# Two spectral and mixer layers in one kernel: a new written-out order of work, one more row summed on ScalarE, smaller first loads

## The chip, the cores and the metric

The kernel runs on one core of a Trainium2 chip. Its engines are TensorE (PE, with its weight loads PEld), VectorE (DVE), ScalarE (ACT), GpSimd (POOL) and SyncE (SP), which here only issues DMAs. The metric is device time of one execution in microseconds (us), the median of several runs.

## The reference

x is 2048 rows of 512 numbers in bfloat16. Two layers, A then B's block, are applied twice with the same weights:

```python
def _A_ref(x, w_r, w_i):
    X = rfft2(x.astype(float32), axes=(-2, -1))
    X = X * (w_r + 1j * w_i)
    return irfft2(X, s=(S, D), axes=(-2, -1)).astype(bfloat16)

def _B_ref(x, w1, w2, w3, w4):
    h = gelu(layernorm(x) @ w1)            # four quarters of h are shifted by -1, +1, -2, +2 rows
    x1 = x + shifted(h) @ w2
    return x1 + gelu(layernorm(x1) @ w3) @ w4      # 512 -> 1792 -> 512

for _ in range(2):
    x = x + _A_ref(layernorm(x), w_r, w_i)
    x = x + _B_ref(layernorm(x), w1, w2, w3, w4)
```

## The kernel before

Everything stays on the chip: `x_state` holds x as 128 partitions by 16 "rows" of 512 (a row here is one of the 16 values of q, with one sequence position in each partition). The Fourier transforms are matmuls with constant tables. One layer runs through these stages, each a letter in the written-out order, with a number for the row, pair or block, `.k` for the PSUM bank, and a last letter for the engine where there is a choice (A ScalarE, V or D VectorE, P GpSimd):

- Front: `s` statistics of a row, `i` their aggregation, `f` the same from sums made on ScalarE, `S` and `J` the root and its inverse, `Q` the table T times one over the deviation of a row (tile `Tq`), `O` the first transform (L403), `G` and `L` its copy to the tile `V`.
- Spectral part over 16 blocks b: `d` a transform (L544 to L550), `t` its copy (tile `TV`), `q` a transform whose matmuls use 64 rows of the array (L568), `x` its copy (tile `X`), `p` the product with the filter W (tile `PB`; from `X`, or with D straight from PSUM), `b` and `V` the way back (L598), `m` and `l` the copies to `hT`.
- Rest of the inverse: `D` and `C` (L618), `Y` the copy, `P` (L646), `a` the addition to x (L654), `s` squares on ScalarE, then `r`, `e`, `i`, `M` for the next normalization, `n` the normalized row, `T` the DMA that transposes two rows (L674, tile `xT`).
- Mixer: `v` the product with w1 (L686), `h` its Gelu (L693), `u` the product with w2 (L702), `f` the addition, `k` squares, `R`, `o`, `U` the second normalization and its transposing DMA, `w` the product with w3 (L737), `g` its Gelu (L744), `W` the product with w4 (L757), `A` the addition (L763), `y` the store. While the first layer's `W` runs, `B`, `j`, `S`, `Q`, `O`, `G`, `I` already make the second layer's front.
- `X` is a number of matmuls on zeros that keep TensorE going; 30 of them (L262) open the program.

The order is written out by hand in three strings: `ORDER_0` (first front), `ORDER_A` (first layer with the front of the second) and `ORDER_B` (second layer). The program is made in that order, and each engine runs its own instructions in it; semaphores hold an instruction until its operands are there and its buffer or bank is free. The tiles `TV` and `Y` share four buffers, `X` has three, `Tq` eight.

Loads: SP issues x in eight pieces of two rows, then sixteen pieces of W. ScalarE issues the table T and two small strided pieces of W ahead of its first table load. GpSimd issues FL, TL and TR after the `f` of group 2, then, after the last `Q`, four copies W to W (`double(0)` to `double(3)`), the computation of half of TL's second plane (`turn_TL`, L238 and L239), the rest of TL and the second half of TR. SP then waits for the last of these through a small DMA (`gate2`, L209) and loads G, Tinv, w1, w2, w3 and w4, one DMA each, followed by a transposing DMA of zeros (L512). DMAs from SP and ScalarE take eight completion semaphores in turn, so one issued as the ninth waits until the first has landed.

`ON_ACT` lists the rows whose sums ScalarE makes in the first front: two activations with an accumulator (L353, L290) in place of one `bn_stats` (L278) and one `bn_aggr` (L306) on VectorE, followed by three small GpSimd instructions (L359 to L361).

Of the kernel before, what the change touches and what calls it, by code (L numbers as in the profile page):

```python
# [16 lines left out]
P = 128  # L17
# [3 lines left out]
NQ = 16  # L21
# [135 lines left out]
def load_all(K, A_x, A_w_r, A_w_i, B_w1, B_w2, B_w3, B_w4):  # L157
# [11 lines left out]
    table("T", nc.scalar)  # L169
    for h in range(8):  # L170
        nc.sync.dma_start(K.x[:, h * 2:h * 2 + 2, :], xv[:, h * 2:h * 2 + 2, :])
    K.W = K.const.tile([P, 2, NH, 257], BF16, name="W")
    planes = [w.rearrange("(m j) f -> m j f", j=64) for w in (A_w_r, A_w_i)]
    for pl, v in enumerate(planes):
        nc.scalar.dma_start(K.W[2::4, pl, 0], v[:, 32])
    for lo in range(0, NH, 8):
        for pl, v in enumerate(planes):
            load_W(K, v, pl, lo, lo + 8)
# [28 lines left out]
    def load_mlp():  # L207
# [4 lines left out]
        for k, w, n, c in (("w1", B_w1, 4, D), ("w2", B_w2, 4, D), ("w3", B_w3, 4, FH), ("w4", B_w4, 14, D)):  # L212
            t = K.const.tile([P, n, c], BF16, name=k)
            nc.sync.dma_start(t[:], w.rearrange("(t p) n -> p t n", p=P))
# [164 lines left out]
def scaled_T(K, q, r, eng="V"):  # L379

    K.Tq[q] = K.stream.tile([P, 2, P], BF16, name="Tq", bufs=8)
    if eng in "VP":
        e = K.nc.vector if eng == "V" else K.nc.gpsimd
        e.tensor_scalar(K.Tq[q][:], K.T[:], r, None, op0=ALU.mult)
    else:
        K.nc.scalar.activation(K.Tq[q][:], K.T[:], ACT.Copy, bias=0.0, scale=r)  # L386
# [137 lines left out]
def layer(K, last):  # L524
# [264 lines left out]
    def scale_T(n, eng):  # L789
        k, i = divmod(n, 4) if n < 12 else (n, 0)  # L790
        scaled_T(K, ROWS[n], lnA[k].r[:, i:i + 1], eng)
# [54 lines left out]
ON_ACT = [5, 9]  # L846
# [16 lines left out]
s1 s0 i1 i0 S0 s2 s5 J0 Q0A Q1A s4 s7 s6 i4 f2 O0.4 i7 i6 S2 s3 J2 i2 s9 Q6V Q7V O3.0 i3 s11 S1 J1 s10 Q4A Q2A Q5A G3A  # L863
s8 i11 i10 i8 s12 f3 O2.2 Q3P O1.6 S3 J3 Q11P s13 i12 Q10A O5.0 s15 G0A i13 Q8A Q9P S4 G2A s14 i15 J4 Q12V i14 O4.4 S5
J5 Q15V G1A G5V Q13P O6.2 L5A O8.0 Q14V O7.6 G4A G6V G7A L7A G8V L6V L8V
"""
ORDER_A = """
d2.2 t2V d0.6 t0A d1.0 d4.4 N0 q0.6 t1A q2.2 d6.0 x0V p0V q1.6 t4A q4.4 x2A d10.2 t6A d8.0 p1D b1.6 p2P t10A b0.7
q10.2 p4D m0V t8A q6.0 d14.4 m1A d12.6 x10A t14V p10V x6A d15.2 t12A p6V b2.5 b4.3 m4A q14.0 q12.6 x14A q8.3 p12D b3.0
m2A b10.1 b11.5 x8A b7.4 t15A p14P q15.2 b5.6 b14.7 m10A b6.1 m11A b12.5 m7A m5A m3A b13.4 m6A p8V b8.6 m12A p15D b9.0  # L870
m8A b15.2 m15A V12.1 m13V V13.3 l12A m14V V15.4 V14.5 m9V l15V D3.0 l14V D1.6 l13A C1 C3 D0.2 C0 Y1A P3.4 P2.5 Y0A Y3V
a3 s3 P6.0 a2 s2 P1.1 P0.6 a1 a0 s1 P7.2 D2.4 C2 D5.6 s0 a7 s7 D7.2 C5 Y2V P5.1 r0 e0 i0 a6 Y5A a5 D4.4 s6 s5 P4.0 M0
# [61 lines left out]
```

## Time and profile before

| | us |
|---|---|
| median of 3 runs | 345.87 (345.47 to 346.12) |
| profiled execution | 346.01 |
| its span, first to last instruction | 344.2 |
| TensorE busy in the span | 335.5 |
| ScalarE busy | 195.6 |
| VectorE busy | 165.0 |
| GpSimd busy | 107.1 |

The span is 1.81 us shorter than the execution; this part lies around the instructions. Busy time of TensorE contains the zero matmuls, and the ends of matmuls are modelled. The granted TensorE clock of the execution is 1.000. A "wait" of an engine is idle time put down to the semaphore that came last.

### The profile page before, as it was taken

How to read it: one execution, taken by the hardware profiler on the slowest of the kernel's cores; microseconds unless marked ns; L12 is line 12 of the kernel's file. 1: busy time of each engine (PE TensorE's matmuls, PEld its weight loads, DVE VectorE, ACT ScalarE, POOL GpSimd, SP SyncE). 2: the span in 40 equal slices, each digit the busy share in tenths (PEclk: the TensorE clock that was granted, in tenths of full speed). 3: DMA queues.
4: the chain of work that ended last, by engine and by line, in shares of the span. 5: the costliest groups of instructions: out<-in, count | busy, mean ns of one | idle time of the engine just before them, and what ended most of it. 6: DMA issues, size and time to landing. Idle time of an engine off the chain costs nothing.

```text
span 344.2 us, 5699 instructions
## 1 busy us (share of the span) xinstructions
PE 335.5 (97%) x2171; PEld 187.6 (55%) x2189; DVE 165.0 (48%) x377; ACT 195.6 (57%) x357; POOL 107.1 (31%) x200
## 2 busy tenths in 40 slices
PE   7999999999999999999999999999999999999996
PEld 5878974444444444454467888444444444444443
DVE  4889895685035015264676979647802000110122
ACT  4979899768752403534538979968681446014300
POOL 2884066668242000304011404765591000000000
PEclk9999999999999999999999999999999999999999
DMA  7986986333030100300000002541403500000121
GB/s 257 314 295 230 372 202 113 72 61 62 3 61 0 32 0 0 31 2 0 2 0 2 2 3 47 104 81 20 89 0 76 109 0 0 30 18 5 41 78 46
DMA packets 45259, 24.60 MB, mean 71 GB/s; under 512 B 35072, under 2 KB 42240, under 8 KB 45232
## 3 DMA queue, kind: packets, MB, share of 16 engines
q1 hardware_dynamic: 43760, 19.74, 23.5%
q0 software_dynamic: 1232, 4.40, 3.7%
q8 instruction: 17, 0.28, 0.3%
q10 hardware_dynamic: 240, 0.10, 0.1%
q14 instruction: 10, 0.08, 0.1%
HBM read 11.61 MB, written 2.10 MB: 40 GB/s over the span
## 4 chain that ended last, share of the span: by engine, by line
PE 87%; DMA 4%; DVE 4%; ACT 2%; issue 1%; SPq 0%; POOL 0%; ACTq 0%; DVEq 0%; POOLq 0%
PE ps L737 28%; PE ps L757 26%; PE ps L686 8%; PE ps L702 8%; PE ps L598 4%; PE ps L403 3%; PE ps L618 3%; PE ps L568 2%; DMA xT<-xn 2%; PE ps L550 2%; PE ps L646 2%; DMA x_state<-in_A_x_dram 1%; DVE x_state L654 1%; ACT xn L290 1%; ACT gT L744 1%
## 5 line engine op out<-in xcount | busy, mean ns | idle before, releaser
L744 ACT ACTIVATE gT<-ps 128x1024 bf16<-128x1024 f32 x56 | 55.8, 1022 | 86.1 <-PE ps L737 86.1
L737 PE MATMUL ps<-xT,w 128*128 128x512 bf16 x448 | 99.2, 379 | 0.5 <-DMA xT<-xn 0.5
L757 PE MATMUL ps<-w,gT 128*128 128x512 bf16 (+2 forms) x462 | 97.8, 366 | 0.7
L763 DVE TENSOR_TENSOR x_state<-ps,x_state 128x512 bf16<-128x512 f32 (+2 forms) x34 | 22.2, 659 | 124.5 <-PE ps L757 124.5
L757 PEld LDWEIGHTS <-gT 128*128 128x128 bf16 x476 | 45.5, 98 | 51.4
L737 PEld LDWEIGHTS <-w 128*128 128x128 bf16 x448 | 43.7, 98 | 53.1 <-DMA xT<-xn 1.0
L710 DVE SCALAR_TENSOR_TENSOR xn<-xn,ln_c,ps 128x512 bf16<-128x512 bf16 x32 | 23.0, 743 | 15.5 <-PE ps L702 8.8
L686 PE MATMUL ps<-xT,w 128*128 128x512 bf16 x128 | 28.9, 379 | 0.7 <-DMA xT<-xn 0.4
L702 PE MATMUL ps<-w,hT 128*128 128x512 bf16 x124 | 28.3, 379 | 0.2
L290 ACT ACTIVATE junk<-xn 128x512 bf16<-128x512 bf16 x32 | 19.7, 622 | 4.8 <-DVE xn L710 4.8
L278 DVE BATCH_NORM_STATS2 ln_st<-x_state 128x6 f32<-128x512 bf16 (+2 forms) x31 | 20.2, 663 | 3.9 <-DMA x_state<-in_A_x_dram 3.6
L654 DVE SCALAR_TENSOR_TENSOR x_state<-ps,x_state 128x512 bf16<-128x512 f32 x32 | 20.7, 684 | 1.3 <-PE ps L646 1.2
L686 PEld LDWEIGHTS <-w 128*128 128x128 bf16 x128 | 12.3, 98 | 15.9 <-issue 1.7
L702 PEld LDWEIGHTS <-hT 128*128 128x128 bf16 x128 | 12.4, 98 | 15.3 <-ACT hT L693 0.4
L290 ACT ACTIVATE xn<-x_state 128x512 bf16<-128x512 bf16 x32 | 19.8, 620 | 0.9 <-DVE x_state L654 0.7
L693 ACT ACTIVATE hT<-ps 128x512 bf16<-128x512 f32 x32 | 17.4, 601 | 4.6 <-PE ps L686 4.4
L313 POOL TENSOR_SCALAR ln_ve<-ln_mv 128x4 f32<-128x4 f32 x11 | 2.8, 257 | 54.6 <-DVE ln_mv L306 53.9
L646 PE MATMUL ps<-Y,Tinv 128*128 128x256 bf16 x128 | 16.0, 272 | 0.1
L598 PE MATMUL ps<-TR,PB 128*128 128x128 bf16 x256 | 16.0, 219 | 0.0
L584 DVE TENSOR_TENSOR PB<-ps,W 128x1024 bf16<-128x1024 f32 x13 | 15.4, 1217 | 0.7 <-PE ps L568 0.5
L618 PE MATMUL ps<-G,hT 128*128 128x256 bf16 x128 | 15.7, 272 | 0.0
L403 PE MATMUL ps<-Tq,x_state 128*128 128x256 bf16 (+1 forms) x160 | 14.0, 246 | 1.6 <-ACT Tq L386 1.0
(95 smaller groups left out, 405.9 us busy)
## 6 DMA issues: line engine op xcount, KB each, us to landing
w<-in_B_w_dram SPq DMA_DIRECT2D x2, 1792.0 KB, 14.3
W<-W POOLq DMA_DIRECT2D x4, 514.0 KB, 5.0
x_state<-in_A_x_dram SPq DMA_DIRECT2D x8, 256.0 KB, 4.7
out_dram<-x_state SPq DMA_DIRECT2D x15, 128.0 KB, 1.9
w<-in_B_w_dram SPq DMA_DIRECT2D x2, 512.0 KB, 6.2
W<-in_A_w_r_dram SPq DMA_DIRECT2D x7, 128.5 KB, 5.8
W<-in_A_w_i_dram SPq DMA_DIRECT2D x7, 128.5 KB, 5.9
TL<-tab_TL POOLq DMA_DIRECT2D x3, 256.0 KB, 5.4
```

The source lines that it names most:

```text
L290: K.nc.scalar.activation(out, src, ACT.Square, bias=0.0, scale=D ** -0.5, accum_out=self.s[:, i, 1:2])
L403: K.nc.tensor.matmul(dst, lhsT=K.x[:, q, c * P:(c + 1) * P], rhs=rhs, start=(j == 0), stop=(j == 3))
L598: nc.tensor.matmul(o[:, k0 * P:(k0 + 1) * P], lhsT=pab[u][:, k, 2 * (b - u) + h, f * P:(f + 1) * P], rhs=K.TR[:, k:k + 2, 2 * b + h], star ...
L618: nc.tensor.matmul(o[:, i, e * 256:(e + 1) * 256], lhsT=M[:, F, e, 2 * m + i, :], rhs=K.G[:, F, e, :], start=(F == 0 and e == 0), stop=(F ...
L646: nc.tensor.matmul(o[:, h * 256:(h + 1) * 256], lhsT=K.Tinv[:, c], rhs=rhs[:, ::-1] if h else rhs, start=(e == 0), stop=(e == 1))
L654: nc.vector.scalar_tensor_tensor(K.x[:, q, :], ps.pop(("P", q)), 1.0, K.x[:, q, :], op0=ALU.mult, op1=ALU.add, accum_out=ln[g].s[:, i, 0:1])
L686: nc.tensor.matmul(o[:, i], lhsT=K.w1[:, t, j * P:(j + 1) * P], rhs=xT[g][:, :, t, :], start=(t == 0), stop=(t == 3))
L702: nc.tensor.matmul(o, lhsT=K.hT[:, j, st:st + P], rhs=K.w2[:, j, :], start=(j == 0), stop=(j == 3))
L710: nc.vector.scalar_tensor_tensor(xn[:, q, :], xn[:, q, :], ln[q // 4].c[:, q % 4:q % 4 + 1], ps.pop(("u", n)), op0=ALU.mult, op1=ALU.add, ...
L737: nc.tensor.matmul(o[:, i], lhsT=K.w3[:, c, t * P:(t + 1) * P], rhs=xT3[g][:, :, c, :], start=(c == 0), stop=(c == 3))
L744: nc.scalar.activation(gT[g][:, 2 * j:2 * j + 2, :], ps.pop(("w", k)), ACT.Gelu_apprx_tanh, bias=0.0, scale=1.0)
L757: nc.tensor.matmul(o, lhsT=gT[g][:, t, i * P:(i + 1) * P], rhs=K.w4[:, t, d], start=(t == 0), stop=(t == 13))
```

## The change

- x comes in nine pieces: rows 0 and 1 by a DMA each, then pairs.
- The table T is issued by ScalarE after the two strided pieces of W, no longer before them.
- w1, w3 and w4 are loaded in two DMAs each; w2 in one.
- Row 1's sums are made on ScalarE (`ON_ACT` gains 1), so group 0 has an `f` too.
- In the second layer's front, rows whose transform is done without folding (`PLAIN`, the first twelve) need T only with one sign: `Tq` is 128 wide there in place of 256.
- All three orders are written anew. The matmuls are the same, but for the zero matmuls at the head of `ORDER_B`: six in place of three.

```diff
-    table("T", nc.scalar)
-    for h in range(8):
-        nc.sync.dma_start(K.x[:, h * 2:h * 2 + 2, :], xv[:, h * 2:h * 2 + 2, :])
+    for lo, hi in ((0, 1), (1, 2), *((h, h + 2) for h in range(2, NQ, 2))):
+        nc.sync.dma_start(K.x[:, lo:hi, :], xv[:, lo:hi, :])
...
         nc.scalar.dma_start(K.W[2::4, pl, 0], v[:, 32])
+    table("T", nc.scalar)
...
-            nc.sync.dma_start(t[:], w.rearrange("(t p) n -> p t n", p=P))
+            v = w.rearrange("(t p) n -> p t n", p=P)
+            for part in ((slice(0, n),) if k == "w2" else (slice(0, n // 2), slice(n // 2, n))):
+                nc.sync.dma_start(t[:, part], v[:, part])
...
-    K.Tq[q] = K.stream.tile([P, 2, P], BF16, name="Tq", bufs=8)
+    K.Tq[q] = K.stream.tile([P, signs, P], BF16, name="Tq", bufs=8, padded_shape=[P, 2, P])
...
-        scaled_T(K, ROWS[n], lnA[k].r[:, i:i + 1], eng)
+        scaled_T(K, ROWS[n], lnA[k].r[:, i:i + 1], eng, 1 if n < 2 * PLAIN else 2)
...
-ON_ACT = [5, 9]
+ON_ACT = [1, 5, 9]
```

The stretches of the orders that the prediction speaks of, before (-) and after (+):

```diff
 ORDER_0
-s1 s0 i1 i0 S0 s2 s5 J0 Q0A Q1A s4 s7 s6 i4 f2 O0.4 i7 i6 S2 s3 J2 i2 s9 Q6V Q7V O3.0
+s0 s1 i0 s5 s2 s3 s4 i3 i2 f0 S0 S1 i4 J0 Q0A Q1A s7 J1 Q3A O0.5 Q2A O1.0 s6 i7 i6 f2
...
-J5 Q15V G1A G5V Q13P O6.2 L5A O8.0 Q14V O7.6 G4A G6V G7A L7A G8V L6V L8V
+Q13V O5.0 G2A L5V O6.4 Q14P O7.2 G4A G7A G5V Q15V L7A O8.0 G8A G6V L6V L8A
 ORDER_A
-d2.2 t2V d0.6 t0A d1.0 d4.4 N0 q0.6 t1A q2.2 d6.0 x0V p0V q1.6 t4A q4.4 x2A d10.2 t6A d8.0 p1D b1.6
+d2.3 d0.6 d1.2 N0 t2V d4.0 t0A q0.6 t1V q2.4 d6.2 t4A x2A q1.0 p0D t6A d10.6 t10A q4.4 d8.2 t8A p1D
...
-P9.5 n4V a10 s10 P8.4 a8 s8 v1.0 a9 s9 P14.7 a13 s13 h1 v0.4 a14 T2 c0 h0 r2 n8P v3.6 h3 v2.0
+P12.0 T2 a10 a8 a13 s11 n6P s9 s8 n7P s10 P14.5 r2 a14 n9V v1.1 h1 v0.5 a15 T3 h0 s13 v3.1
...
-w15.0 g15 w19.2 g19 B4 w18.0 g18 g17 w20.6 j4 j6 g20 o14A B5 W11.0 j5 S1 U6 Q6V W9.1 Q4P o15P U7 A11 B11 w21.6
+g3 w2.2 g6 U2 E9V o9P R3 w5.6 E14V E15V o15V o14V o10A ... o8A U4 E12V w13.4 g13 o12P U7 W0.6
...
-W12.3 A12 B12 j12 S12 S13 J13 Q13P J12 W15.1 A15 B15 j15 S15 J15 Q15A W14.2 W24.5 Q12A Q10V O5.6 A14 A24 O6.2 G5A B14
-B24 j14 S14 G6A J14 Q14A L6A O15.0 G15A L15A O14.2 G14A G5V I5V L14A
+W14.0 G4V I4P A12 B12 j12 S12 J12 A13 W24.4 Q12A B13 J15 Q15A Q10V j13 S13 J13 A14 A24 B14 O5.2 B24 j14 G5A O15.6 G15A
+L15V Q13P O6.0 S14 J14 Q14A O14.4 G6A L6A G5V G14A L14A I0P I5V
 ORDER_B
-q12.0 x12A d10.2 q8.4 p2D d14.0 p4P b4.1 d6.6 p12V m4V t10A x8A b3.2 b5.5 q10.3 t6A t14A q6.6 m5A b12.0 m3A b2.1 m12A
-b1.5 p8V b8.0 p0P b9.2 x6A b0.6 b15.7 m8A p10D q14.3
+q12.2 x12A q2.0 p4V b5.6 m5A b15.7 m15A t8V q8.4 x8A d10.6 t10A d6.2 p0P b1.4 p2D t6A b4.1 b0.0 m0A p8V q10.6 p12V
+q6.2 b2.0 m1A m4A x6A b8.4 p10D b3.1 b12.5 b9.3 b13.2 p6V q14.6
```

## The prediction

> **What bounds the kernel now.** I read the clock and the page's first part, then what TensorE waits for, then the chain that ended last, then single stretches of the timeline.
>
> ```profile
> PE 335.5 (97%) x2171; PEld 187.6 (55%) x2189; DVE 165.0 (48%) x377; ACT 195.6 (57%) x357; POOL 107.1 (31%) x200
> ...
> PEclk9999999999999999999999999999999999999999
> ```
>
> TensorE is busy 335.5 of 344.2 us at full clock, and the change leaves its real matmuls as they are. So the result can differ only in idle time at TensorE, in what is done before the first real matmul and after the last, and in what TensorE loses between stages. All waits put down to a releaser:
>
> ```profile
> PE ps L403 <- ACT Tq L386: 1.0, 2, 0.8
> PE ps L262 <- DVE zeros L253: 1.0, 1, 1.0
> PE ps L403 <- DVE Tq L384: 0.6, 1, 0.6
> PE ps L568 <- DVE PB L584: 0.5, 1, 0.5
> PE ps L737 <- DMA xT<-xn: 0.5, 1, 0.5
> PE ps L686 <- DMA xT<-xn: 0.4, 1, 0.4
> PE ps L686 <- DVE x_state L654: 0.2, 1, 0.2
> PE ps L546 <- ACT V L154: 0.2, 1, 0.2
> ```
>
> Columns: total us, times, longest. Three of these are single holes in the middle: 0.5 before a `q` of the second layer (waiting for the product in `PB`), 0.5 before a `w` (a transposing DMA), 0.4 before the first `v` (the same). The chain shows where they are, and one cost that is no wait:
>
> ```profile
> 21.85 0.76 PE ps L568 x12
> 22.61 0.16 PE ps L544
> ...
> 48.34 3.29 DMA xT<-xn
> ...
> 142.42 4.57 DMA xT<-xn
> ```
>
> After a group of `q` (64 rows of the array) the next full-height matmul takes 0.16 us where 0.06 is usual at that place; on the way into `q` nothing is lost. The start, from the timeline:
>
> ```profile
> 5.96 0.61 ACT L353 ACTIVATE junk<-x_state 128x512 bf16<-128x512 bf16 x1
> ...
> 7.19 0.89 ACT L386 ACTIVATE Tq<-T,ln_r 128x256 bf16<-128x256 bf16 x2
> ...
> 7.73 1.48 PE L403 MATMUL ps<-Tq,x_state 128*128 128x256 bf16 x16 [0.84 <-ACT Tq L386]
> ```
>
> The first real matmul starts at 7.73, 0.54 after ScalarE begins the first `Tq`, and ScalarE was with row 5's sums just before.
>
> **The change part by part,** against the profiled execution (span 344.2, time 346.01, which is 0.14 above the median 345.87).
>
> *Start: +0.1.* Rows 0 and 1 landed together 3.5 us after their issue at 0.72, at 4.2. In halves, with T behind, I estimate row 1 at 4.0. ScalarE is ready at 3.94 (after its table load). `s1` there is two activations at 0.61 with reads, 1.23 in pitch: 4.0 to 5.25. Next in its queue is `s5`, whose rows land at 5.9 as before (the same 768 KB plus T and the small W pieces precede them): 5.9 to 7.15. Only then come S0 and S1 (0.28 each), though f0 on GpSimd (0.19 + 0.28 + 0.24) ended near 6.0. So Q0A starts at 7.65 and TensorE at 8.2, 0.45 later than before. But before there was a hole of 0.57 between the first pair of rows and the second; the new order takes rows 2 and 3 next, whose `Tq` follow on ScalarE without a break. The 128 matmuls of the front take 10.9 us (1.48 + 9.44): 8.2 + 10.9 + about 0.2 of small waits is 19.3 against 19.2. Bounds: -0.4 (row 5 lands before 5.3), +0.9 (ScalarE's own load, about 1.2 more from `s1`, decides to the end). T is needed at 7.6, its landing 3.2 after an issue near 2.05: hidden. The piece with rows 8 and 9 now waits for the first strided W piece (about 4.0) where the piece with rows 10 and 11 waited for T; needed at 9.3, hidden by two us. W's sixteen pieces are issued about 0.5 later on SP, but the last three waited for landings before, so the last lands near 22 as before. VectorE is relieved of 0.66 + 0.15 for row 1; it isn't what S0 waits for.
>
> *GpSimd's queue: 0.* The last `Q` is now row 15 on VectorE, behind a copy of V; I place it at 18.2 where the last one began at 17.3 (S5 on ScalarE at 16.0 behind two copies of V, its inverse 0.16, row 13's `Q` 0.3, then two copies of 0.68 on VectorE), and its end at 18.5 against 17.6. Part of that is caught up, because the first copy W to W used to wait for W's landings; so `turn_TL` and everything behind it on GpSimd, four W copies and two table DMAs, comes 0.5 later by my count, and so do SP's gate and the w loads. Second half of TR: landed 7.9 after its issue at 23.26, so 31.2, then 31.7 to 31.9; its first user is now `b11`, which TensorE reaches at 31.9. Covered by 0.1 only.
>
> *Two more ways out of `q`: +0.25.* ORDER_A has seven such places, before five; ORDER_B six and six. Row: 0.10 to 0.16 each. The Trainium skill, "TensorEngine Tiling (Array Packing)", Key Properties, says that changing the tiling mode drains TensorE. Read so, in and out both cost and I would count four drains, +0.6; the row shows only the way out dear. I take the row.
>
> *First `v`: 0.* The first group's `n` for rows 0 and 1 are both on GpSimd now, its DMA goes first, the other's 1.3 (SP's time for one) later; it lands at about 51.7, as before. TensorE comes 0.44 later, because the last `P` stands ahead of `v1`. So the 0.4 goes. But `v3.1` reuses a bank of `v1.1`, so it needs the first Gelu, behind the table load (1.28, before it ended at 55.45), and rows 6 and 7, whose `n` are two of GpSimd at 0.76 behind row 4's (first at 50.0, done 52.3, two DMAs to issue, 3.1 to landing): I get 55.8 for both against 55.45 when TensorE comes. +0.4 back. Bounds -0.4 and +0.5.
>
> *The hole before `w21`: -0.5.* It waited for U7, whose `o14A` stood behind three Gelus (1.02 each). Now `o14V` and `o15V` come some 40 us before their use.
>
> *Between the layers: +0.1.* After the last piece of `W`: A 0.29, two `B` 0.67, `j` 0.2, root 0.3, inverse 0.16, `Q` 0.5, against O5, O15, O6 (0.45, 0.68, 1.35) on TensorE; as before. After O14 two more copies of 0.6 stand ahead of the last two of 0.38 on ScalarE, so V is complete 0.1 later; the six zero matmuls (0.11 each) fill the wait. Bounds -0.1, +0.4.
>
> *Second layer's spectral part: -0.45.* Before, q14 waited 0.5 for a product on VectorE (1.22 each half); now p10D ends 0.2 before q14 is reached, by adding VectorE's pieces from its first one (185.7) on. Working: TensorE starts `d15` at 184.0; until q14 stand 16 blocks of `d` at 0.33, 15 of `q` at 0.25, 8 and three halves of `b` at 0.45, and five ways out of `q`: 14.0, so 198.0. VectorE starts p15D at 185.7; nine pieces (t 0.69, t8 1.22, p 1.22 a piece, 2.44 where PSUM is read for two blocks) make 12.9, less 0.1 overlap each, with 0.2 of waits: 197.8. VectorE's whole load grows from 16.2 to 17.4 here (p4V in place of GpSimd's, t8V in place of ScalarE's). Bounds -0.5, +0.6.
>
> *Second layer's `P` to `v`: -0.1* (the waits of 0.2 and 0.1 for VectorE's additions to free a bank; bounds -0.2 and +0.2); `y` and the last store: 0, the tail ends with the same pieces.
>
> *Loads of w in halves: 0.* Three more issues at 0.5 on SP. The Trainium skill, "DMA: Bandwidth & Descriptors", Measured, advises at least 1 MiB per DMA and gives a fixed cost of about 2 us in its section Anatomy of one DMA. If that were paid in series, w4 would land up to 6 us after its 49.3, and the transposes behind it would hold `v1`. The row speaks against it: x's 256 KB pieces, 3.5 to 5.3 us each to landing, came in while the first three slices of the page moved 257 to 314 GB/s, so the fixed parts overlap. The narrower `Tq` shortens twelve instructions by at most their whole 0.3 to 1.0, on engines that TensorE doesn't wait for there: 0.
>
> Sum: 0.1 + 0.25 + 0 - 0.5 + 0.1 - 0.45 - 0.1 = -0.6. Some ten of the new orders' covers are 0.2 us or less by these sums (b11, q14, t8, d10, b5), so I give back 0.2: -0.4, so 345.5 against the median. Measurement can tell about 0.2% (0.7 us) from no change.
>
> **The rivals.**
> 1. *Everything holds (faster):* row 5 lands early, no thin cover breaks, `v3` isn't late: -0.4 + 0.25 - 0.4 - 0.5 - 0.5 = -1.5, 344.4. For it: the holes named are real and single. Against: ScalarE's queue at the start has no room.
> 2. *GpSimd's chain comes late (slower):* if row 15's `Q` starts after 18.6, the second half of TR comes after 32.2 and `b11` waits one for one; w4 and the first transposes come later by the same, since both hang on the gate. With 19.3 for that `Q`: +0.9 at `b11`, +0.5 at `v1`, 347.0. For it: one chain of DMAs with no slack at its end; ScalarE's load before it grows. Against: TensorE's own start shifts too and takes part of it.
> 3. *VectorE becomes the bound of the spectral stages:* it gains 0.85 us in the first (t1 and m6, m7, m15 for it, x0 and p15's half from PSUM off it) and 1.2 in the second, in stretches of 20 us where it was busy 17.6 and 17.0. If half of it shows: +1.0 in place of the cover, 346.6. A product ran 2.20 in place of 1.22 while GpSimd made one too.
>
> **How the numbers follow.** My sum 0.45 (345.0 to 346.2), rival 1 0.2, rival 2 0.2, rival 3 0.15. Faster: rival 1 and a third of my case, 0.35; slower: most of rival 2, half of 3 and a few of mine, 0.3; the rest 0.35. Range: 344.3 to 347.2.
>
> **What would show it.** TensorE's waits: no wait of 0.5 before a `w` and none before `q14`; one before a `v` near 55.5; the first real matmul near 8.2 and the first `d` near 19.7. Rival 2: a wait of TensorE at the `b` line for a TR load. Wrong outright if TensorE's busy time grows by more than 0.7 beside the added zeros.

## The result and the profile after

| | before | after |
|---|---|---|
| median of 20 executions each, us | 346.04 | 344.74 (344.00 to 347.01) |
| ratio after to before, 95% interval | | 0.9976 [0.9964, 0.9989] |
| profiled execution, us | 346.01 | 344.21 |
| its span, us | 344.2 | 342.4 |
| TensorE busy in the span, us | 335.5 | 334.2 |

The changed kernel is faster: 1.30 us by the medians, 0.83 by the ratio on record (which is not the quotient of the two medians, 0.9962), 1.80 by the two profiled executions. The profiled execution of the changed kernel is the third fastest of its 20, that of before lies at its median; so the stages below show somewhat more than the usual gain. The page after, busy times and the clock:

```profile
PE 334.2 (98%) x2175; PEld 186.9 (55%) x2192; DVE 163.1 (48%) x370; ACT 195.2 (57%) x360; POOL 108.7 (32%) x210
...
PEclk9999999999999999999999999999999999999999
```

TensorE's busy time did not grow. What it waits for (total us, times, longest):

```profile
PE ps L405 <- DMA x_state<-in_A_x_dram: 2.8, 1, 2.8
PE ps L264 <- DVE zeros L255: 1.0, 1, 1.0
PE ps L600 <- DVE PB L586: 0.3, 1, 0.3
```

Three lines stand where eight stood. The holes before a `q`, before a `w` and before the first `v` are all gone; one of 0.3 before a `b` is new (its place is shown below); and the start has a wait of 2.8 where 0.84 was. That first line is the one to remember: it costs little where it stands, and yet it matters.

I cut both profiled executions at the first matmul of each stage. The columns are the length of each stretch before and after, and the difference:

| stretch | before | after | difference |
|---|---|---|---|
| start to first `d` | 19.36 | 19.54 | +0.18 |
| first `d` to first `D` | 17.70 | 18.19 | +0.49 |
| `D` to first `v` | 14.70 | 14.53 | -0.17 |
| first `v` to first `u` | 7.34 | 7.15 | -0.19 |
| `u` to first `w` | 20.79 | 20.72 | -0.06 |
| `w` to end of the last `W` | 99.80 | 99.13 | -0.68 |
| between the layers, to `d` of the second | 3.95 | 3.69 | -0.25 |
| second layer, `d` to `D` | 18.36 | 17.87 | -0.50 |
| `D` to `v` | 14.47 | 14.28 | -0.19 |
| `v` to `u` | 7.17 | 6.96 | -0.20 |
| `u` to end of the last `W` | 117.61 | 117.67 | +0.05 |
| last `W` to the end of the span | 2.98 | 2.70 | -0.28 |

The differences add up to -1.80 (rounded). The front of the first layer and its spectral part lost 0.67; the stages after it gained, but for the last `u` to `W`, which is the same within 0.05.

The start after, engines' rows from the timeline (start, duration, engine, line, operation, and in brackets the idle time before it and what ended it):

```profile
5.33 1.88 DVE L280 BATCH_NORM_STATS2 ln_st<-x_state 128x6 f32<-128x512 bf16 x3 [1.42 <-DMA x_state<-in_A_x_dram]
...
6.36 0.63 ACT L355 ACTIVATE junk<-x_state 128x512 bf16<-128x512 bf16 x1 [1.05 <-DMA x_state<-in_A_x_dram]
...
7.60 0.46 ACT L367 ACTIVATE ln_r<-ln_mv,eps 128x2 f32<-128x2 f32 x2
...
8.11 1.30 ACT L388 ACTIVATE Tq<-T,ln_r 128x256 bf16<-128x256 bf16 x3
...
8.67 0.49 PE L405 MATMUL ps<-Tq,x_state 128*128 128x256 bf16 x4 [2.76 <-DMA x_state<-in_A_x_dram]
```

ScalarE waits 1.05 us for rows 4 and 5 (second row), makes row 5's sums, and only then takes S0 and S1 (third row) and the first `Tq`. TensorE's first real matmul starts at 8.67.

The new hole, and the two old ones that went:

```profile
33.36 0.39 PE L570 MATMUL ps<-TV,TL 64*128 64x256 bf16 x4
34.04 1.17 PE L600 MATMUL ps<-TR,PB 128*128 128x128 bf16 x18 [0.29 <-DVE PB L586]
```

Before, `q14` had the hole: a gap of 0.53 ahead of the `q` at 198.38. After, the last `q` of the second layer follows its `b` without a gap:

```profile
194.90 2.52 PE L600 MATMUL ps<-TR,PB 128*128 128x128 bf16 x40
197.35 0.39 PE L570 MATMUL ps<-TV,TL 64*128 64x256 bf16 x4
197.67 2.53 PE L600 MATMUL ps<-TR,PB 128*128 128x128 bf16 x41
```

And in the chain that ended last, TensorE's products with w1 run from 52.26 with one short break at the third `v`, where the prediction had feared a wait of 0.4:

```profile
49.41 2.79 PE ps L648 x24
52.26 3.61 PE ps L688 x16
55.96 3.61 PE ps L688 x16
```

One thing is not in this profile. The mean granted TensorE clock was 0.999 or 1.000 in 14 of the 20 executions (344.00 to 346.19, median 344.53), and 0.995 in the other six (345.58 to 347.01, median 346.18). For the kernel before, 176 executions that ran beside the experiments have a clock on record: none is below 0.999. So the change brought something that makes a third of its executions 1.65 us longer. The experiments on the clock look for it.

### The profile page after: what moved, and what is told of

The parts are those of the page before. It is cut to its first block, busy times and chain, and to the rows that moved or that the text cites. A ratio compares the mean times of both kernels' runs of the same rounds, so it can differ in the third digit from the quotient of the medians.

```text
span 342.4 us, 5725 instructions
## 1 busy us (share of the span) xinstructions
PE 334.2 (98%) x2175; PEld 186.9 (55%) x2192; DVE 163.1 (48%) x370; ACT 195.2 (57%) x360; POOL 108.7 (32%) x210
## 4 chain that ended last, share of the span: by engine, by line
PE 93%; DMA 2%; DVE 2%; issue 1%; ACT 1%; SPq 0%; DVEq 0%
PE ps L739 28%; PE ps L759 28%; PE ps L688 8%; PE ps L704 8%; PE ps L648 4%; PE ps L620 4%; PE ps L405 4%; PE ps L600 3%; PE ps L552 2%; PE ps L570 2%; DMA x_state<-in_A_x_dram 1%; PE ps L415 1%; DMA W<-in_A_w_r_dram 1%; PE ps L546 1%; PE ps L548 1%
## 5 line engine op out<-in xcount | busy, mean ns | idle before, releaser
L280 DVE BATCH_NORM_STATS2 ln_st<-x_state 128x6 f32<-128x512 bf16 (+2 forms) x30 | 19.4, 664 | 3.8 <-DMA x_state<-in_A_x_dram 3.5
L600 PEld LDWEIGHTS <-PB 128*128 128x128 bf16 x256 | 14.5, 98 | 1.9 <-issue 1.7
```

The source lines that it names most:

```text
L600: nc.tensor.matmul(o[:, k0 * P:(k0 + 1) * P], lhsT=pab[u][:, k, 2 * (b - u) + h, f * P:(f + 1) * P], rhs=K.TR[:, k:k + 2, 2 * b + h], star ...
```

## The experiments

### The parts of the change, one at a time

Four kernels ran beside 62 executions of the kernel before (median 346.24).

*The new loads alone*, put into the kernel before (x in nine pieces, T later, w1, w3 and w4 in halves):

```diff
-    table("T", nc.scalar)
-    for h in range(8):
+    for lo, hi in ((0, 1), (1, 2), *((h, h + 2) for h in range(2, NQ, 2))):
...
+    table("T", nc.scalar)
...
+            for part in ((slice(0, n),) if k == "w2" else (slice(0, n // 2), slice(n // 2, n))):
```

> The kernel before with the new loads alone (rows 0 and 1 by a DMA each, T after the strided W pieces, w1, w3 and w4 in halves); its orders stay. Theory (the loads as such move nothing that ends a stage): rows 0 and 1 land near 3.4 in place of 4.2, but the first Tq stands on ScalarE behind row 5's sums, whose rows land later (6.3 in place of 5.9), so the first real matmul comes at 7.7 to 8.2, the first d at 19.2 to 19.6, and the time is within 0.3 us of before. Rival (the loads carry the gain): the first real matmul comes 0.7 us earlier and the time falls by 0.5 us or more. Second rival (halves cost): w4 and the first transposes come later, the wait before the first v grows from 0.4 to 1 us or more.

Median 345.25, ratio 0.9976 [0.9964, 0.9989]: as much as the whole change by itself. Its stages say where from. The first `d` comes 0.34 sooner (19.02), which one profile can't tell from chance (a later kernel with the same loads and front has it at 19.38). The first `v` comes 0.27 later than before, after a wait of 0.67 for its transposing DMA, and a new wait of 0.87 for another stands before the first `v` of the second layer. What is gained is the end of the program after the last `W`, 0.28 shorter (explained further down), and the hole before `w21`, which is gone, though U7 leaves no earlier there (142.64, before 142.42): the stretch from `w` to the last `W` takes 99.13 in place of 99.80. U7's DMA landed 3.04 us after its issue in this kernel and 4.57 in the kernel before. The hole before a `q` of the second layer stays (0.52).

*The new front with the new loads* (order up to the first `d`, and row 1 on ScalarE):

```diff
-ON_ACT = [5, 9]
+ON_ACT = [1, 5, 9]
 ORDER_0
-s1 s0 i1 i0 S0 s2 s5 J0 Q0A Q1A s4 s7 s6 ...
+s0 s1 i0 s5 s2 s3 s4 i3 i2 f0 S0 S1 i4 J0 Q0A Q1A s7 J1 Q3A ...
```

> The kernel before with the new loads, row 1 on ScalarE and the new ORDER_0; both layers' orders stay. Theory (stages add up): as in the changed kernel the first real matmul comes near 8.7, the first d near 19.5 (0.2 later than before), then every stage keeps its length: 0.1 to 0.4 us slower than before. Rival (the new front is where the gain comes from): faster by 0.5 us or more.

Median 346.47, ratio 1.0019 [1.0003, 1.0034]. The new front is not better than the old one: the first `d` is at 19.72, 0.70 later than with the loads alone. And 10 of its 22 executions ran at a clock of 0.995 (347.08 to 349.57), against 1 of 15 with the loads alone. At full clock its median is 346.0, 0.7 over the loads alone. The hole before `w21` is absent in its profile too, with the old order of that stage (U7 landed 3.73 us after its issue).

*The new order of the first layer alone* (with the loads and front of before):

```diff
 ORDER_A
-d2.2 t2V d0.6 t0A d1.0 d4.4 N0 q0.6 ...
+d2.3 d0.6 d1.2 N0 t2V d4.0 t0A q0.6 ...
```

> The kernel before with ORDER_A of the changed one alone (Tq keeps both signs in the second front). Theory (stages add up): from the first d to the first d of the second layer 0.8 us less: 0.3 to 0.5 more to the first D, 0.3 less from there to the first u, 0.6 less in the w stage (no wait of 0.5 for a transposing DMA), 0.2 to 0.3 less between the layers; time 0.5 to 1.0 us under before. Rival (the narrow Tq makes the step between the layers shorter): that step stays as before, gain 0.3 us less.

Median 345.07, ratio 0.9971 [0.9962, 0.9981], none of 16 at a lower clock. In the profiled execution the first `D` comes 0.48 later and the first `v` waits 1.14, while the stretch from the first `w` to the last `W` gives 0.67 back. So this order's gain is after the first `w`, and what stands ahead of it is a cost. How much of the gain by the median this explains is open: the profiled execution, at 345.80, is the second slowest of the 16 and only 0.2 us under the profiled one of before.

*The new order of the second layer alone:*

```diff
 ORDER_B
-X3.4 d4.1 d15.0 t15V d12.5 d1.7 t4A ...
+X6.6 d15.2 d1.1 d4.4 t15A q15.6 p15D ...
```

> The kernel before with ORDER_B of the changed one alone (six zero matmuls at its head). Theory (stages add up): the spectral part of the second layer is 0.5 us shorter (no wait for PB before q14), the way to the first u another 0.3 to 0.4; time 0.6 to 1.0 us under before. The three more zero matmuls cost up to 0.3, since V is complete later in the kernel before than TensorE needs. Rival (the gain hangs on the order of the blocks at the first layer's end): 0.2 us or less.

Median 345.51, ratio 0.9980 [0.9970, 0.9989], none of 22 at a lower clock. From `d` to `D` it gains 0.65. The hole of 0.52 to 0.53 before `q` of the second layer is in all the profiles above that have the old order of that layer, and in neither this one nor the changed kernel. The hole before `w21` is here too (0.66).

### The copy o14

One letter in the first layer's order of the kernel before: the copy whose rows U7 transposes goes from ScalarE, behind three Gelus, to VectorE.

```diff
-w15.0 g15 w19.2 g19 B4 w18.0 g18 g17 w20.6 j4 j6 g20 o14A B5 W11.0 j5 S1 U6
+w15.0 g15 w19.2 g19 B4 w18.0 g18 g17 w20.6 j4 j6 g20 o14V B5 W11.0 j5 S1 U6
```

> The kernel before with one letter changed in the first layer's order: the copy o14 goes from ScalarE, where it stands behind three Gelus, to VectorE, as in the changed kernel; nothing else moves. Theory A (the step of the prediction on the hole before the w at 21): the transposing DMA U7 leaves about 2 us earlier, the hole of 0.5 us is gone, the time 0.4 to 0.5 shorter (345.6, ratio 0.9985). Rival B: the hole came from the DMA's slow landing (4.57 us in before, with a 16 KB instruction fetch in its flight, against 3.0 to 3.1 of others): even so 2 us earlier would cover 1.5 us of delay, so the hole goes under both; but if the time doesn't fall by 0.4, TensorE's next wait or VectorE took the 0.5 us up again within the layer. Rival C: the copy on VectorE delays VectorE's elementwise work at the same place by its 0.3 to 0.6 us, and the time stays at 346.0.

Median 345.37 beside 346.05, ratio 0.9985 [0.9977, 0.9993]: -0.5 us. U7's row before and in this kernel:

```profile
142.42 1.23 SPq L674 DMA_TRANSPOSE xT<-xn  x1
```

```profile
140.53 1.23 SPq L674 DMA_TRANSPOSE xT<-xn  x1
```

It leaves 1.89 us earlier, no wait of TensorE before a `w` is left, and the stretch from `w` to the last `W` is 99.13, the same as in the changed kernel. In the profiles this one letter gives all that the change gains there.

But the hole needed a second condition: of the five profiles with the old letter in the old order, only two have it. In the kernel before, a 16 KB transfer of the instruction queue starts at 144.09, in U7's flight, and U7 takes 4.57 us where the median of the 32 transposes is 3.13. In the kernel with the second layer's order alone the transfer starts at 143.61 and U7 takes 4.72 (the hole is there); with the new front and loads it starts at 143.60, U7 takes 3.73, and there is no hole; with the new loads alone it starts at 146.61, U7 takes 3.04, and there is none; and so with 22 zero matmuls (below: 146.85, 3.10). So the letter makes the stage safe from a slow landing that comes in a part of the kernels. The page's queue rows of the changed kernel show how few such transfers there are:

```profile
q8 instruction: 17, 0.28, 0.4%
```

Columns: transfers, MB, share of the 16 engines. Seventeen transfers for the 4367 matmuls and weight loads of that page (2175 and 2192) is one in about 257 of them; so which DMA a transfer meets hangs on where the program's instructions happen to stand.

The traces let one ask how far this holds. In all fourteen profiles together 366 transposing DMAs were issued after 60 us. In seven of them a 16 KB transfer started 0.25 to 2.0 us after the issue, and these landed after 3.65 to 4.72 us, five of them after more than 4.3. The other 359, among them 25 that met a transfer nearer to their start or their end, took at most 3.68. Every landing of over 3.8 us had a transfer there; no run took the transfer away alone.

### The clock

*The kernel before with 22 zero matmuls at the start in place of 30:*

```diff
-WAKE = 30
+WAKE = 22
```

> The kernel before with 22 zero matmuls at the start in place of 30 (nothing else changed): the idle time before the first real matmul grows from 0.84 to about 2.5 us, as long as in the changed kernel, while order and loads stay those of before. Theory A (idle time alone sets the dip of the clock): executions at a granted clock of 0.995 now occur in before too, in a fifth to a half of them, each some 1.5 to 3 us longer; the median rises by 0.3 to 1.5, and the profiled first real matmul stays at 7.7. Rival B (the dip belongs to the new orders): all executions stay at 1.0 and the ratio is 0.999 to 1.001. Rival C: with fewer zero matmuls the clock rises later in every execution: all are longer by 0.2 to 1, with no two groups.

Median 347.35, ratio 1.0038 [1.0021, 1.0054]. Nine of 18 executions had a clock of 0.989 to 0.995, in a kernel with the old loads and the old orders throughout. So it is not the new orders; and since the changed kernel lost clock with the full 30 zero matmuls, what the two share is the longer idle time ahead of the first real matmul. The profiled execution, at full clock:

```profile
4.61 1.27 PE L262 MATMUL ps<-zeros 128*128 128x256 bf16 x5
7.65 0.60 PE L403 MATMUL ps<-Tq,x_state 128*128 128x256 bf16 x5 [1.76 <-ACT Tq L386]
```

*The changed kernel with 44 zero matmuls:*

```diff
-WAKE = 30
+WAKE = 44
```

> The kernel after with 44 zero matmuls at the start in place of 30 (nothing else changed). In the runs of the changed kernel 6 of 20 executions had a mean granted TensorE clock of 0.995, and were 1.3 to 3 us longer than the others; none of some 62 of the kernel before had it. Theory A: the clock drops for one window because TensorE stands idle for 2.76 us between the last zero matmul (5.91) and the first real one (8.67); 14 more zero matmuls end at 7.4 to 8.9 and leave an idle time under 1.3 us, so the executions at 0.995 should be gone or nearly so (0 to 1 of 15), the fast ones unchanged at 344.0 to 344.4, the median about 344.2 and the ratio to before 0.994 to 0.996. Rival B: the dip comes from elsewhere in the new orders (the boundary between the layers, say): a third of the executions stay at 0.995 and the median at 344.7. Rival C: the added zero matmuls run past the first real transpose and delay it by 0.2 to 0.5: no 0.995, but all executions 0.2 to 0.5 longer.

Half right. One execution of 11 ran at 0.995 in place of 6 of 20. But the median was 347.47 and the ratio 1.0044 [1.0029, 1.0058]: slower than before, at full clock. The waits of TensorE of its profiled execution, its fastest:

```profile
PE ps L688 <- DVE x_state L656: 1.4, 1, 1.4
PE ps L264 <- DVE zeros L255: 1.0, 1, 1.0
PE ps L405 <- ACT Tq L388: 1.0, 1, 1.0
```

The 1.4 stands before the third `v` of the second layer, and VectorE had long been done there. Two transposing DMAs are under way just before:

```profile
214.16 1.55 SPq L676 DMA_TRANSPOSE xT<-xn  x1
```

```profile
215.83 1.87 SPq L676 DMA_TRANSPOSE xT<-xn  x1
```

They landed 4.50 and 4.36 us after these starts (the changed kernel: 3.28 and 3.18), and their issue took 1.55 and 1.87 where 1.23 to 1.34 is usual. The instruction queue's 16 KB transfer, at 219.93 in the changed kernel, starts at 216.08 here, in their flight; what stands ahead of it in TensorE's queue differs by fourteen matmuls with their weight loads. This accounts for the profiled execution (span 344.1 against 342.4, 1.39 of it the hole). The median of this kernel's other executions at full clock is another 1.6 us longer; no profile shows what they lost, and the explanation of the hole does not reach it.

*The changed kernel with 30 zero matmuls of 384 columns* in place of 256: as long as 44 of the old width, with the number of instructions unchanged.

```diff
-    fill(K, WAKE)
+    fill(K, WAKE, 3)
...
-0:256], lhsT=K.zeros[:], rhs=K.zeros[:].unsqueeze(1).to_broadcast([P, 2, P])
+0:c * P], lhsT=K.zeros[:], rhs=K.zeros[:].unsqueeze(1).to_broadcast([P, c, P])
```

> The kernel after with its 30 zero matmuls 384 columns wide in place of 256: they last half as long again (0.32 us each before the clock rises, 0.16 after), end at 7.3 to 8.8 and leave under 1.4 us before the first real matmul, as 44 of the old width did; but the number of TensorE's instructions stays that of after. Theory A (two causes: the idle time sets the dip of the clock; the 1.39 us hole ahead of a v in the kernel with 44 came from a 16 KB instruction fetch that 14 more matmuls moved from 219.9 to 216.1, into the flight of two transposing DMAs, which landed after 4.4 to 4.5 us in place of 3.2): no or hardly any execution at 0.995 (0 to 2 of 15), no transposing DMA over 4 us near 215, no hole over 0.3 in the second layer, all executions at 344.0 to 344.9, median 344.4, ratio 0.9945 to 0.996. Rival B (more work at the start costs by itself, whatever the fetches): clock near 1.0 but the executions 1.5 to 3 longer, 346 to 348, as with 44. Rival C (the first real matmul is held back by the zeros): 0.1 to 0.4 longer than after's best, 344.4 to 344.8.

Median 344.92 (344.59 to 345.62), ratio 0.9961 [0.9949, 0.9974], none of 9 executions below 0.999, no transposing DMA over 4 us near 215. So the longer zeros do not cost by themselves. What else set the kernel with 44 apart is its number of TensorE instructions; how that made most of its executions slow is shown for the hole of the profiled one alone. The zeros run up to the first real matmul:

```profile
7.25 1.46 PE L264 MATMUL ps<-zeros 128*128 128x384 bf16 x8
8.72 0.98 PE L405 MATMUL ps<-Tq,x_state 128*128 128x256 bf16 x10
```

Its best execution is 0.6 above that of the changed kernel, and the profile shows a new hole of 1.09 before the first `v`:

```profile
49.01 4.22 DMA xT<-xn
...
53.36 0.81 PE ps L688 x3
```

(the chain: the second transposing DMA landed 4.22 us after its issue.)

### The first transposing DMAs, and the rest

That hole appeared in other kernels too. Over the profiles the wait before the first `v` was 0.40 (before), under 0.1 (after), 0.67 (new loads alone), 1.14 (first layer's order alone), 1.16 (before, 22 zero matmuls), 1.09 (the last kernel). In the six profiles with the first layer's old order the first `d` lies anywhere from 18.95 to 19.72, but the first `v` only from 51.75 to 52.11, and the earliest `d` has the latest `v`: in five of these six `v` waits for a DMA, and an earlier front gains nothing there. What is behind it?

*The changed kernel with w1, w3 and w4 whole:*

```diff
-            for part in ((slice(0, n),) if k == "w2" else (slice(0, n // 2), slice(n // 2, n))):
-                nc.sync.dma_start(t[:, part], v[:, part])
+            nc.sync.dma_start(t[:], w.rearrange("(t p) n -> p t n", p=P))
```

> The kernel after with w1, w3 and w4 loaded whole again (four loads in place of seven). The prediction put the halves at 0. Theory A: 0: the landing of w4 moves by under 0.5 us, T0 and T1 land in time for the first u, and the time is 344.0 to 344.9 with the stage starts of after within 0.1. Rival B: the halves matter because SyncE's queue holds the transposing DMAs behind them: with whole loads the first transposes go out earlier or later by up to 2 us and the wait ahead of the first v (0.09 in the changed kernel, 0.67 with the new loads in the old order) changes by 0.3 to 0.6, the time with it.

Median 345.74, ratio 1.0002 [0.9983, 1.0021]: the gain was not seen any more. w4 landed at 50.55 (48.93 in the changed kernel), the first transposing DMA at 52.20 (51.48), and the first `v` waited 0.38. But this kernel's first real matmul also came 0.43 later, behind rows 4 and 5 that landed 0.43 later (6.77) in a queue that is the same up to there, and 5 of its 14 executions were below a clock of 0.999. The loads of w started 0.93 later as well (32.34). Counted from the first of these loads to the landing of w4, whole loads took 16.4 to 18.2 us in six profiles, and halves 16.8 to 20.1 in seven; so nothing here shows that the halves are faster, and the loss of this run can't be put down to the whole loads.

*The changed kernel with the front of before* (order and `ON_ACT`):

```diff
-ON_ACT = [1, 5, 9]
+ON_ACT = [5, 9]
```

> The kernel after with the front of before (the order up to the first d, and row 1's sums on VectorE); the new loads, the one-signed tables and the orders of both layers stay. Theory A (the parts add up: at full clock the new loads were worth -0.8, the new front +0.6 and a clock dip in up to half of the executions, layer one -1.0, layer two -0.55): the first d comes at 19.0 in place of 19.54, the executions fall to 343.5 to 344.3, none or hardly any at 0.995, the median 343.9, ratio 0.993 to 0.995. Rival B (the order of layer one was made for the new front: what it needs first is late from the old one): the first d comes earlier, but q and b wait 0.3 to 0.6 more, and the median is 344.4 to 344.9. Rival C (the earlier end of the front is taken back by the loads ahead of the first v, as in the kernel with the new loads alone, where the wait there grew to 0.67): the first v comes no sooner than in after, and the median is 344.3 to 344.6, without dips.

Median 345.15, ratio 0.9980 [0.9968, 0.9991]. The parts do not add up as theory A had them. The first `v` waited 1.92 in the profiled execution:

```profile
PE ps L688 <- DMA xT<-xn: 2.2, 2, 1.9
PE ps L405 <- ACT Tq L388: 1.6, 1, 1.6
```

w4's second half landed at 51.16 and the first transposing DMA at 52.92, after SyncE had been held 3.10 us in issuing it. And 7 of 19 executions were at 0.994 to 0.995.

*The changed kernel with row 5's sums moved behind Q1A:*

```diff
-s0 s1 i0 s5 s2 s3 s4 i3 i2 f0 S0 S1 i4 J0 Q0A Q1A s7
+s0 s1 i0 s2 s3 s4 i3 i2 f0 S0 S1 i4 J0 Q0A Q1A s5 s7
```

> The kernel after with ScalarE's sums of row 5 (s5) moved behind Q1A, so that S0, the square root that the first Tq needs, no longer stands behind the landing of rows 4 and 5. Theory A (the step Start: s5 made the first real matmul 8.67 in place of 8.2): the first real matmul comes at 8.0 to 8.3; the first d does not move by more than 0.1 (19.5), since what is late there is the load of W and the fold of V, and the time at full clock stays at 344.0 to 344.9. The idle time falls from 2.76 to about 2.2, and executions at 0.995 stay (1 to 5 of 15). Rival B: the first d comes 0.4 earlier as well, and the time falls by as much. Rival C: row 5's scaled table is now late, TensorE waits for it within the front, and the first d comes 0.3 later.

Median 346.23, ratio 1.000 [0.9989, 1.0010]: rival C. The first real matmul came at 8.58, hardly sooner, two holes opened in the front, and the first `d` came at 21.32 (19.54 in the changed kernel):

```profile
8.58 1.48 PE L405 MATMUL ps<-Tq,x_state 128*128 128x256 bf16 x16 [1.82 <-DMA x_state<-in_A_x_dram]
11.00 3.46 PE L405 MATMUL ps<-Tq,x_state 128*128 128x256 bf16 x40 [0.94 <-ACT Tq L388]
15.07 1.15 PE L405 MATMUL ps<-Tq,x_state 128*128 128x256 bf16 x12 [0.61 <-ACT Tq L388]
```

S0 ran at 6.01, early as expected. But S1 stands ahead of Q0A as well, and it started at 7.84: it needs VectorE's statistics of rows 2 to 4 and their aggregation, which begin when rows 2 and 3 have landed; in the changed kernel they run from 5.33 to 7.42. In this execution VectorE could begin only at 5.78, since rows 2 and 3 landed later, so the 0.1 gained is too small a figure for the move: with VectorE's start of the changed kernel, 0.45 earlier, Q0A and TensorE would have begun some 0.5 us before those of the changed kernel (an estimate from these times). The two holes behind it are what made the run slow.

*The wide zeros, and w4's second half issued behind the last transposing DMA of the first layer's first mixer half:*

```diff
+        if k == 6 and not last:
+            K.load_w4()
```

> The kernel with the 384-column zero matmuls (30 of them), and w4's second half issued on SyncE behind the last transposing DMA of the first layer's first MLP half (about 66 us) in place of ahead of the first (w4 is first read at 99). Over ten profiles so far the wait ahead of the first v was 0.0 to 1.9 us; where the last part of w4 landed at 50.5 to 51.2 the first transposing DMA landed 1.65 to 1.76 after it, at 52.2 to 52.9. Theory A (the tail of w4's load sets the landing of the first transposes): with only w4's first half ahead of them (it lands at 46 to 47) the first lands at 50.7 to 51.2, the second by 52.2, the wait ahead of the first v is under 0.2 us, the profiled span 342.1 to 342.6, no execution at 0.995, all at 343.8 to 344.5, median 344.2, ratio 0.993 to 0.9955. Rival B (the first transposes are slow by themselves, whatever is ahead of them): the first still lands 4.2 to 5 us after its issue in some runs, the wait stays at 0.4 to 1.9, and the executions stay at 344.6 to 345.6. Rival C: the moved load now runs into the transposes of the first layer's second MLP half or the load of nothing else, a hole of 0.3 or more appears ahead of a w near 80 to 100, and the time is no better than 344.9.

Median 344.94, ratio 0.9970 [0.9959, 0.9981], 2 of 22 at 0.995. No wait before the first `v` was left, as theory A had it, but TensorE was late by then: the copy W to W that GpSimd issued at 17.58 landed at 23.41 (22.16 in the changed kernel), VectorE's first product began at 23.58 (22.49 in the changed kernel, 0.33 after the landing there), and a `d` waited for the product:

```profile
PE ps L549 <- DVE PB L589: 0.8, 1, 0.8
```

The first transposing DMA took 3.79 us with only half of w4 ahead of it. This run does not settle what makes it slow, and the version is no better than the changed kernel. None of the twelve is shown to beat it: the two with wide zeros and the first layer's order alone (0.9971) have lower ratios, but their intervals overlap its own.

## Why the prediction was right, and where it was not

The forecast was 345.5 (-0.4), the result is 344.74, close to the first rival (344.4), which kept every gain and paid nothing at the third `v`. The single holes that it named are gone, and that is the mechanism it had right. The size is less well founded: the gain was two to three times the -0.4 foreseen, most terms came out lower by up to 0.4 and one higher by 0.24, and the clock, which no term had, took back 0.5 in the mean (6 of 20 times 1.65). Step by step:

- *Start, +0.1: not contradicted, but one pair can't tell.* The first `d` moved by +0.18 to 19.54. Over the profiles it lies at 18.95 to 19.65 with the old front and loads (five), and at 19.54 to 19.97 with the new (six); the middle of the two differs by 0.3. (The first `d` near 19.7 that was named as a sign is not 0.1 above 19.36 either.) The first real matmul came at 8.67, not 8.2: row 1 landed at 3.38, earlier than the 4.0 assumed, but rows 4 and 5 at 6.34 rather than 5.9, and VectorE's statistics, which the step set aside as not what S0 waits for, hold S1 until 7.42, 0.3 before `s5` ends (7.69). As foreseen, the front then ran without its hole: 128 matmuls in 10.72.
- *GpSimd's queue, 0: right.* The last `Q` began at 18.00 (18.2 foreseen), the second half of TR landed at 31.48 (31.7 to 31.9), and no `b` waited for it. The second rival, with its chain of late loads, did not come.
- *Two more ways out of `q`, +0.25: mis-sized, from a wrong reading of the rows.* The way into `q` is not free. It stands inside the groups of `q` in the chain of before:

```profile
186.01 0.76 PE ps L568 x12
...
187.87 0.32 PE ps L568 x4
...
190.96 0.54 PE ps L568 x8
...
193.99 0.98 PE ps L568 x16
```

Four matmuls more add 0.22 each time, so 0.10 of every group goes with its start. From start to start of the matmuls it is 0.20 from a `d` into `q`, where 0.11 is usual behind that `d`, and 0.20 on the way out, where 0.11 is usual: 0.10 each way, at nearly every change in all fourteen profiles. So the reading with four drains, which the prediction set aside, was the right one, at 0.10 each: two more groups of `q` cost 0.40. From `d` to `D` the first layer lost 0.49: 0.40 for this, and about 0.3 for the hole before a `b` at 34.04, for a product on VectorE, with smaller waits of before gone. That hole is a thin cover that broke, of the kind the 0.2 given back was for.
- *First `v`, 0: wrong.* The 0.4 before `v` went as said (under 0.1 is left), but the 0.4 at the third `v` did not come: it started at 55.96 after a gap of 0.09. From `D` to `u` the changed kernel gains 0.36 in the profiled execution. Rows 6 and 7 landed at 55.83, as worked out (55.8). What failed is the 55.45 for TensorE: it came 0.50 later than before to the first `v` and was free for the third at 55.87, so the cost was already paid. The experiments add that the first wait varies between under 0.1 and 1.92 among kernels with nearly the same queue, and that `v` starts at 52.26 to 54.12 in the eight profiles with the first layer's new order, the changed kernel's being the earliest; so its profile was lucky here, and this term should have had a far wider bound.
- *The hole before `w21`, -0.5: right*, and shown alone: -0.5 us by the ratio for the one letter, and the stage's 0.68 whole in its profile. But the hole is absent from three of the five profiles with the old letter, so that it was there to be removed is in part luck. What the step missed is why U7 was late by so much: a landing of 4.57 us with an instruction transfer in its flight. At 3.1 it would have landed 1.5 earlier, and the hole would have been covered in the old order too.
- *Between the layers, +0.1: mis-sized.* It measured -0.25. From the last `W` to the zero matmuls it is 3.04 in place of 3.45: the last eight matmuls of `O` had waited for a `Tq` before, and no longer do. That wait shows as an idle time of 0.21, but from the start of the matmul ahead of it to the start of the one behind it 0.48 passed where 0.11 is usual, so it cost 0.37, nearly all of the 0.41. The three zero matmuls more cost 0.15, and the `d` follows them without a gap.
- *Second layer's spectral part, -0.45: right.* -0.50, the hole before `q14` gone, and -0.65 with that order alone. VectorE ended the product p10D at 197.19 and TensorE reached q14 at 197.35, a cover of 0.16 where 0.2 was worked out. VectorE as a bound (the third rival) did not show there; in the first layer it showed as 0.29.
- *Second layer's `P` to `v`, -0.1: mis-sized.* `D` to `u` gained 0.39.
- *The tail, 0: wrong.* It is -0.28, and it is the change's. The last store lands equally soon after the last matmul (1.79 us, before 1.82). But SyncE asks for its eight completion semaphores one after the other, in a fixed order, 0.06 us each. Before, four more follow the one of the last store; in the changed kernel that one is the last. The four more DMAs of the new loads turned the semaphores on by four places. In the seven other kernels with these loads the stretch is 2.70 to 2.72, in the four others with the old loads 2.96 to 2.98, and with whole loads of w, one more DMA than before, 2.89 with three more semaphores to ask.
- *Loads of w in halves, 0: right against the price.* The rule weighed there would have put w4 up to 6 us later (the page gives its figures for DMAs that GpSimd issues, these come from SyncE); it landed at 48.93, 0.36 sooner than whole before. With whole loads in the new order it landed 1.6 later, 0.9 of it a later start. Over all profiles halves took 16.8 to 20.1 us and whole loads 16.4 to 18.2, so neither is shown to be faster.
- *What the sum left out: the clock.* Every step assumed TensorE at full clock. A longer idle time at the start was priced at its own length and found to be hidden. It was hidden, and yet with it 6 of 20 executions were 1.65 us longer.

## What to carry to other kernels

Price idle time of TensorE ahead of the first real work twice: for its own length, and for the clock that it may lose; keep the warm-up matmuls going until the real ones start (wider ones did it here without the slow executions that more of them brought), and look at the clock of every execution, not of the one in the profile. Where a hole waits for a DMA, ask first whether the DMA was slow or its issue late: an earlier issue makes the kernel insensitive to a slow landing, and that is worth having even where the slow landing is chance. Gains of parts measured alone (the loads and the two orders, -0.7 to -1.2 each by the medians) need not add: the hole before `w21` is gone from the profile of the loads alone and from that of the first layer's order alone, and it can go only once. And where a term is read off a trace, read from start to start: the ends of matmuls are modelled, and an idle time of 0.21 cost 0.37 here.

## What the runs showed of the hardware

*The clock.* Ordered by the place of the first real matmul and the idle time ahead of it in the profiled execution, with the executions at a clock below 0.999:

| kernel | first real matmul | idle ahead | lower clock |
|---|---|---|---|
| first layer's order alone | 7.53 | 0.28 | 0 of 16 |
| second layer's order alone | 7.67 | 0.31 | 0 of 22 |
| before | 7.73 | 0.84 | 0 of 176 |
| o14 on VectorE | 7.50 | 1.69 | 0 of 21 |
| new loads alone | 8.01 | 1.28 | 1 of 15 |
| before, 22 zero matmuls | 7.65 | 1.76 | 9 of 18 |
| after, old front | 8.34 | 1.61 | 7 of 19 |
| new loads and front | 8.86 | 1.71 | 10 of 22 |
| after, `s5` late | 8.58 | 1.82 | 2 of 14 |
| after | 8.67 | 2.76 | 6 of 20 |
| after, whole w | 9.10 | 3.37 | 5 of 14 |
| after, 44 zero matmuls | 8.93 | 0.99 | 1 of 11 |
| after, wide zeros | 8.72 | none | 0 of 9 |
| wide zeros, w4 behind | 8.91 | 0.73 | 2 of 22 |

The idle time of one profile is not that of every execution: in the profiled ones full clock begins anywhere from 3.7 us (whole w) to 7.0 (the second layer's order alone), in the changed kernel at 4.0, and a zero matmul takes 0.21 us before that and 0.11 after, so 30 of them end anywhere from 5.7 to 7.4. Taken from the earliest end, 5.7, the kernels with 30 narrow zero matmuls and an idle time of up to 2.0 show no lower clock in 235 executions; those that can reach 2.6 or more show it in 30 of 89 (the new loads alone, at up to 2.3, in 1 of 15). The Trainium skill, "TensorE: Matmul & The Clock Gate", Part 1: The HAM clock gate, has a free-running window of 3413 ns and half the clock after an idle one. By that page half a clock for one window would take, as an estimate, 3.4 x 0.5 = 1.7 us; a mean of 0.995 over 344 us is 0.005 x 344 = 1.7 us, and 1.65 is what the executions lost; so the size fits one such window. The window's length shows in the traces as well: in the twelve profiles with a record of it full clock lasts 337.9 us in ten and 341.3 in two, 3.4 apart. The page's rule warns of idle gaps over about 3.4 us; here, as far as the earliest end of the zeros seen (5.7) holds for every execution, gaps of at most 2.6 to 3.4 are enough in a part of them. When in the execution the window came was not seen, since all the profiled executions ran at 0.999 or 1.000. The three lower ones among the 42 executions with the idle time wholly or mostly filled are not explained.

*The instruction queue.* A 16 KB transfer of it that starts 0.25 to 2.0 us after the issue of a transposing DMA goes with landings of 3.65 to 4.72 us (seven of seven), where at most 3.68 is seen otherwise (359), and its place moves by microseconds with a few instructions more or less. Two kernels that differ only in how many zero matmuls they run at the start so differed by a hole of 1.4 us at 219 us. That the transfer is the cause is argued from where it stands. The first transposing DMAs, ahead of 60 us, are slow without one too (4.9 us with the wide zeros).

*Half-height matmuls.* A group of matmuls on 64 rows of the array costs TensorE 0.10 us on the way in and 0.10 on the way out, in all fourteen profiles.

*The end of the program.* Each semaphore that SyncE still has to ask for behind the landing of the last store adds 0.06 us; four fewer of them go with 0.28 of this change's 1.80.
